# One query against 65,536 keys on one core: second pair's values in three parts, odd pairs' outer stretches in one pass, output rows turned by VectorE

## The chip, the cores and the metric

The kernel runs on one core of a Trainium2 chip. The core has five engines that run side by side and meet through semaphores: TensorE (PE in the profile, with its weight loads as PEld), VectorE (DVE), ScalarE (ACT), GpSimd (POOL) and SyncE (SP). SP does no arithmetic here; it issues the DMA transfers that bring keys and values from device memory (HBM). The transfers are carried by 16 DMA engines. The metric is the device time of one execution in microseconds; lower is better.

## What is computed

The reference is grouped-query attention for a single query position (decode). There are 32 query heads and 8 key/value heads; four query heads share one key/value head.

```python
B, Hq, Hkv, Sq, Sk, D = 1, 32, 8, 1, 65536, 128
k = jnp.repeat(k, 4, axis=1)          # each kv head serves 4 query heads
v = jnp.repeat(v, 4, axis=1)
scores = jnp.einsum("bhqd,bhkd->bhqk", q, k) * D ** -0.5
p = softmax(scores, axis=-1)
out = jnp.einsum("bhqk,bhkd->bhqd", p, v)
```

Keys and values are 134 MB each in bf16 and each byte is used for one small product, so every byte has to be read once: 268.44 MB in all.

## The kernel before, in words

**Units and pairs.** The keys of one head are cut in two halves, and the kernel works on one half at a time. It calls a half a *pair*; there are 16 pairs (`NR`), two per head, numbered i = 0 to 15. A pair has 256 rows of keys per partition (`2 * T`), 8 MiB of keys and 8 MiB of values. It is handled as two units of `A` = 160 and `C` = 96 rows; a unit has its own softmax maximum, and later units rescale the accumulated result.

**The keys of a pair** (`pe_keys`). TensorE transposes the 256 rows in 32 blocks of 8 (L139). VectorE evicts two blocks of three from PSUM to SBUF, ScalarE the third (L240, L238). TensorE multiplies the transposed keys with the queries (L157). As soon as the first 20 blocks have been evicted, `kfree` is raised (L236) and SP may load the next pair's keys. VectorE takes the maximum (L275), GpSimd spreads it over the partitions (L440), ScalarE makes the exponentials (L403).

**The values of a pair** (`pe_values`). TensorE multiplies exponentials and values in three *stretches* (`stretch`, L184): stretch 0 is rows 0 to 96, stretch 1 (the middle one) rows 96 to 160, stretch 2 rows 160 to 256. Each adds up in a PSUM place of its own (`vsum`). Stretch 1 goes first. The two outer stretches follow in a loop of two passes (L200): in even pairs 0 and then 2, in odd pairs 2 and then 0, because the 160-row unit, whose exponentials are ready first, covers stretches 0 and 1 in even pairs and 1 and 2 in odd ones. Ahead of each stretch TensorE waits for a count of `exd` (exponentials done). Each outer stretch raises `pvd`; when both have come, VectorE raises `vfree` (L321), adds the stretches to the accumulator `acc`, and SP may load the next pair's values.

**Small TensorE work in the values.** At the head of `pe_values` TensorE transposes the finished heads' outputs (`oT`, L198), and in the second pass it sums the softmax denominators with a column of ones (L204). Both are done in every pair; only the results of the last pair are used, by VectorE at the end (L381 and L383).

**SyncE's order** (`sync_engine`). Pair 0: keys in three parts, values in one. Pair 1: `load_both(1, 1)`, that is, wait for `kfree`, load the keys, wait for `vfree`, load all values in one transfer (L469 to L473). Pairs 2 to 13: the same in a loop. Pair 14: keys and values in two parts each. Pair 15: keys in three parts, values in eight (`V_PIECES`: 48, 24, 12, 6, 4, 2 rows for stretch 0). There is one value buffer, so a pair's values can be loaded only where the previous pair's have been used. The transfers of SP's queue are carried out in their order of issue. Semaphores `vrdy[0]`, `vrdy[1]` and `vpiece[...]` tell TensorE which part has landed; where a pair is loaded in one transfer, SP raises the others itself.

**The end** (`vector_engine`, L379 to L391). After the last pair VectorE copies the transposed rows of the earlier heads (`orow`), which ScalarE stores; it takes the reciprocal of the denominators, adds stretches 1 and 2, rescales, waits for stretch 0, adds it; TensorE transposes `acc` (L213); VectorE scales it into `olast` (L389), and SP stores it (L502).

Of the kernel before, what the change touches and what calls it, by code (L numbers as in the profile page):

```python
# [5 lines left out]
DT = mybir.dt  # L6
AF = mybir.ActivationFunctionType
ALU = mybir.AluOpType
AX = mybir.AxisListType

P = 128


T = 128
C = 96
A = 2 * T - C
# [25 lines left out]
def take(e, sem, n=1):  # L42

    e.wait_ge(sem, n)
    e.sem_inc(sem, -n)  # L45


def bass_standalone__gqa_softmax__decode_kernel(nc, q, k, v, out):
    _, Hq, _, D = q.shape
    _, H, Sk, _ = k.shape  # L50
    R = Hq // H
    HR = H * R
# [18 lines left out]
    def sb(name, shape, dt):  # L71
        return S(nc.sbuf_tensor(name, shape, dt))

    def sem(name):
        return S(nc.semaphore(name))
# [10 lines left out]
    row = sb("row", [P, 32], DT.float32)  # L86
    ident = sb("ident", [P, P], DT.bfloat16)
    identf = sb("identf", [P, P], DT.float32)
    ones = sb("ones", [P, 1], DT.float32)
    cmax = sb("cmax", [P, R], DT.float32)  # L90
    cmaxa = sb("cmaxa", [P, R], DT.float32)
    m = [sb(f"m{i}", [P, R], DT.float32) for i in range(2)]
# [8 lines left out]
    rl = sb("rl", [R, 1], DT.float32)  # L101
    oT = sb("oT", [P, HR], DT.float32)
    otmp = sb("otmp", [P, HR], DT.float32)
    orow = sb("orow", [HR - R, D], DT.bfloat16)
    olast = sb("olast", [R, D], DT.bfloat16)
    dscr = sb("dscr", [P, 2], DT.float32)

# [1 line left out]

    qkb = [S(nc.psum_tensor(f"qkb{i}", [P, (2 - i) * BANK], DT.float32)) for i in range(2)]  # L110
    pvb = S(nc.psum_tensor("pvb", [P, BANK], DT.float32))
    fin, finl = pvb, qkb[1]

    vsum = (qkb[0][:, 2 * BANK - R:2 * BANK], pvb[:, 0:R], pvb[:, R:2 * R])

    krdy = [sem(f"krdy{i}") for i in range(len(K_PARTS))]
    vrdy = [sem(f"vrdy{i}") for i in range(2)]
    vpiece = [sem(f"vpiece{i}") for i in range(len(V_PIECES))]
    kfree, vfree = sem("kfree"), sem("vfree")
    trd, tra, evd, eva = sem("trd"), sem("tra"), sem("evd"), sem("eva")  # L120
    qkd, qrdy, pvd = sem("qkd"), sem("qrdy"), sem("pvd")
    cm, cma, ng, exd, sx, lrd, lra = (sem(n) for n in ("cm", "cma", "ng", "exd", "sx", "lrd", "lra"))
    xd, xa, xg = sem("xd"), sem("xa"), sem("xg")
    q_sem, o_sem, s_x, t_z, t_id, t_if, t_qT = (
        sem(n) for n in ("q_sem", "o_sem", "s_x", "t_z", "t_id", "t_if", "t_qT"))
    s_o, t_row, s_l, t_acc, s_fin, t_last = (
        sem(n) for n in ("s_o", "t_row", "s_l", "t_acc", "s_fin", "t_last"))

# [33 lines left out]
    def pe_keys(pe, i):  # L164
        for j in range(GA + LAG):
            if j < GA:
                pe_transposes(pe, j, C + j * TB)
            if j >= LAG:
                pe_scores(pe, j - LAG)

        with pe.If(i % 2 > 0):
            for j in range(GA, G):
                pe_transposes(pe, j, j * TB - A)
        with pe.If(i % 2 < 1):
            for j in range(GA, G):
                pe_transposes(pe, j, C + j * TB)
        for j in range(GA, G):
            pe_scores(pe, j)

    def stretch(pe, q):  # L180
        a, b = ((0, C), (C, A), (A, 2 * T))[q]
        starts = [sum(V_PIECES[:n]) for n in range(len(V_PIECES))] if q == 0 else []
        for r in range(a, b):
            ins = pe.matmul(vsum[q], lhsT=vbuf[:, r * D:(r + 1) * D], rhs=pts[:, r * R:(r + 1) * R],  # L184
                            start=r == a, stop=r == b - 1)
            if r in starts:
                ins.wait_op(vpiece[starts.index(r)], 16, "sem-ge")
        if q != 1:
            ins.then_inc(pvd, 1)

    def pe_values(pe, i):

        take(pe, vrdy[0], 16)
        take(pe, exd)

        pe.transpose(qkb[0][0:HR - R, 0:P], oT[:, R:HR], identf[:, :]).then_inc(s_o, 1)  # L198
        stretch(pe, 1)
        with pe.Fori(0, 2) as s:  # L200
            take(pe, exd)
            with pe.If(s > 0):

                pe.matmul(finl[0:R, 0:1], lhsT=lp[:, :], rhs=ones[:, :],  # L204
                          start=True, stop=True).then_inc(s_l, 1)
            with pe.If((i + s) % 2 > 0):
                take(pe, vrdy[1], 16)
                stretch(pe, 2)
            with pe.If((i + s) % 2 < 1):
                stretch(pe, 0)  # L210

    def pe_last(pe):
        ins = pe.transpose(fin[0:R, 0:P], acc, identf[:, :])  # L213
# [30 lines left out]
    def own(e, ins, s):  # L244
        ins.then_inc(s, 1)
        take(e, s)

    def chain(e, *steps, settle=True):

        for n, make in enumerate(steps):  # L250
            ins = make()
            if n:
                ins.wait_op(xd, n, "sem-ge")
            if settle or n < len(steps) - 1:
                ins.then_inc(xd, 1)
        if settle:
            take(e, xd, len(steps))
        else:
            e.sem_inc(xd, 1 - len(steps))
        return ins  # L260
# [107 lines left out]
    def vector_engine(e):  # L368
        identities(e)
        e.memset(dm[0][:, :], 0.0)  # L370
        own(e, e.memset(oT[:, :], 0.0), xd)
        e.wait_ge(s_x, 1)
        own(e, e.tensor_copy(qT[:, :], trb[0][:, 0:HR]), xd)
        next_queries(e, t_qT)
        e.sem_inc(qrdy, 1)
        with e.Fori(0, H) as h:
            for i in range(HALVES):
                dve_round(e, i, h)
        chain(e, rescaled(e, NU - 2))  # L379
        e.wait_ge(s_o, NR)  # L380
        e.tensor_copy(orow[:, :], qkb[0][0:HR - R, 0:P]).then_inc(t_row, 1)  # L381
        e.wait_ge(s_l, NR)
        e.reciprocal(rl[:, :], finl[0:R, 0:1])  # L383
        take(e, pvd)
        chain(e, added(e, 1), added(e, 2), rescaled(e, NU - 1))
        ins = added(e, 0)()
        ins.wait_op(pvd, 1, "sem-ge")
        ins.then_inc(t_acc, 1)
        ins = e.tensor_scalar(olast[:, :], fin[0:R, 0:P], rl[:, 0:1], None, ALU.mult)  # L389
        ins.wait_op(s_fin, 1, "sem-ge")  # L390
        ins.then_inc(t_last, 1)  # L391
# [25 lines left out]
    def scalar_engine(e):  # L417
        e.dma_start(qsb[:, :], qf).then_inc(q_sem, 16)
        e.wait_ge(t_z, 1)
        e.activation(dscr[:, 1:2], dscr[:, 0:1], AF.Exp, scale=1.0)  # L420
        with e.Fori(0, H):
            for i in range(HALVES):
                act_round(e, i)
        e.wait_ge(t_row, 1)
        e.dma_start(of[0:HR - R, :], orow[:, :]).then_inc(o_sem, 16)


    def gpsimd_engine(e):
        e.memset(ident[:, :], 0.0)
        e.memset(identf[:, :], 0.0)  # L430
        e.memset(ones[:, :], 1.0)
        e.memset(dscr[:, :], 0.0)
        e.memset(la[:, :], 0.0).then_inc(t_z, 1)
        e.wait_ge(t_z, 1)
        e.partition_all_reduce(cmaxa[:, :], la[:, :], P, bass.bass_isa.ReduceOp.max).then_inc(xg, 1)
        e.wait_ge(xg, 1)
        with e.Fori(0, H):
            for _ in range(HU):
                take(e, cm)
                e.partition_all_reduce(cmaxa[:, :], cmax[:, :], P, bass.bass_isa.ReduceOp.max).then_inc(cma, 1)  # L440
            take(e, lrd)
            e.partition_all_reduce(la[:, :], lp[:, :], P, bass.bass_isa.ReduceOp.add).then_inc(lra, 1)
# [5 lines left out]
    def sync_engine(e):  # L448
        kp, vp = pairs(kf), pairs(vf)

        def cols(a, b):
            return slice(a * D, b * D)

        def load_k(i, odd, split=(0,)):

            for n, f in enumerate(split):
                last = (split + (len(K_PARTS),))[n + 1]
                a, b = K_PARTS[f], (K_PARTS + (2 * T,))[last]
                r = row_tile(odd, a) if b - a < 2 * T else 0
                t = r if odd else C + r  # L460
                e.dma_start(kbuf[:, cols(t, t + b - a)], kp[i][:, cols(r, r + b - a)]).then_inc(krdy[f], 16)
                for x in range(f + 1, last):
                    e.sem_inc(krdy[x], 16)

        def load_v(i, ready, a, b):
            e.dma_start(vbuf[:, cols(a, b)], vp[i][:, cols(a, b)]).then_inc(ready, 16)

        def load_both(i, odd):
            take(e, kfree)  # L469
            load_k(i, odd)  # L470
            take(e, vfree)
            load_v(i, vrdy[0], 0, 2 * T)
            e.sem_inc(vrdy[1], 16)  # L473

        load_k(0, 0, (0, 1, 2))
        load_v(0, vrdy[0], 0, 2 * T)

        for sm in [vrdy[1]] + vpiece:
            e.sem_inc(sm, 16)
        load_both(1, 1)  # L480
        with e.Fori(1, H - 1) as h:
            load_both(2 * h, 0)
            load_both(2 * h + 1, 1)
        i = NR - 2
        take(e, kfree)
        load_k(i, 0, (0, 2))
        take(e, vfree)
        load_v(i, vrdy[0], 0, A)
        load_v(i, vrdy[1], A, 2 * T)
        i = NR - 1  # L490
        take(e, kfree)
        load_k(i, 1, (0, 1, 2))
        take(e, vfree)
        for sm in vpiece:
            e.sem_inc(sm, -16)
        load_v(i, vrdy[0], C, 2 * C)
        load_v(i, vrdy[1], 2 * C, 2 * T)
        r = 0
        for n, sm in zip(V_PIECES, vpiece):
            load_v(i, sm, r, r + n)  # L500
            r += n
        ins = e.dma_start(of[HR - R:HR, :], olast[:, :])  # L502
        ins.wait_op(t_last, 1, "sem-ge")
        ins.then_inc(o_sem, 16)
        e.wait_ge(o_sem, 32)
# [35 lines left out]
```

## Time and profile before

| | us |
|---|---|
| three runs: median (lowest to highest) | 632.05 (631.78 to 632.28) |
| the profiled execution, its own time | 632.92 |
| its span, first to last instruction | 630.9 |
| busy in the span: PE | 497.2 |
| PEld | 490.3 |
| DVE | 283.4 |
| ACT | 235.5 |
| POOL | 16.5 |

The profile comes from one execution. Its own time is 2.0 us longer than its span, which begins with the first instruction and ends with the last; the 2.0 us lie outside of what the profile shows. The mean clock granted to TensorE was 0.763 of full speed. HBM was read at 425 GB/s over the span. In timeline rows the first number is the start in us from the span's start, the second the length of the row (of all its instructions together), and the bracket at the end gives how long the engine sat idle before it and what ended the wait ("PEq" and "DVEq" are the engine's own sequencer, "issue" a wait for nothing that the profile shows). In rows of DMA issues the last number is the time from issue to landing.

### The profile page before, as it was taken

How to read it: one execution, taken by the hardware profiler on the slowest of the kernel's cores; microseconds unless marked ns; L12 is line 12 of the kernel's file. 1: busy time of each engine (PE TensorE's matmuls, PEld its weight loads, DVE VectorE, ACT ScalarE, POOL GpSimd, SP SyncE). 2: the span in 40 equal slices, each digit the busy share in tenths (PEclk: the TensorE clock that was granted, in tenths of full speed). 3: DMA queues.
4: the chain of work that ended last, by engine and by line, in shares of the span. 5: the costliest groups of instructions: out<-in, count | busy, mean ns of one | idle time of the engine just before them, and what ended most of it. 6: DMA issues, size and time to landing. Idle time of an engine off the chain costs nothing. (4 is left out here: it accounts for less than half of the span.)

```text
span 630.9 us, 27120 instructions
## 1 busy us (share of the span) xinstructions
PE 497.2 (79%) x12338; PEld 490.3 (78%) x12338; DVE 283.4 (45%) x661; ACT 235.5 (37%) x466; POOL 16.5 (3%) x50
## 2 busy tenths in 40 slices
PE   4764994949859498695976969679596895989897
PEld 4664984949859498694976969679596885989897
DVE  4340553615536054461733517355172543646363
ACT  2240441604425044251533515335152451625353
POOL 0000000000000000000000000000000000000000
PEclk9775886958869588695966859678596786958697
DMA  9998999999999999999999999999999999999996
GB/s 376 437 439 352 465 399 465 399 465 399 461 403 461 403 465 399 465 399 465 399 465 399 465 415 449 432 432 445 420 449 415 461 403 461 395 446 417 432 424 284
DMA packets 6587, 268.59 MB, mean 426 GB/s; under 512 B 818, under 2 KB 1202, under 8 KB 1458
## 3 DMA queue, kind: packets, MB, share of 16 engines
q1 hardware_dynamic: 6488, 268.44, 98.8%
q8 instruction: 7, 0.11, 0.1%
q10 hardware_dynamic: 90, 0.02, 0.0%
q14 instruction: 2, 0.02, 0.0%
HBM read 268.44 MB, written 0.01 MB: 425 GB/s over the span
## 5 line engine op out<-in xcount | busy, mean ns | idle before, releaser
L139 PE MATMUL trb<-ident,kbuf 128*128 128x128 bf16 x4096 | 304.1, 237 | 94.3 <-PEq L45 88.6
L139 PEld LDWEIGHTS trb<-ident,kbuf 128*128 128x128 bf16 x4096 | 272.0, 108 | 95.8 <-issue 95.4
L238 ACT ACTIVATE ktb<-trb 128x1024 bf16<-128x1024 bf16 x176 | 180.2, 1024 | 354.3 <-PE trb L139 347.8
L240 DVE COPY ktb<-trb 128x1024 bf16<-128x1024 bf16 x336 | 221.9, 688 | 157.9 <-PE trb L139 154.3
L157 PE MATMUL qkb<-qcur,ktb 128*128 128x4 bf16 x4096 | 132.4, 164 | 0.7 <-issue 0.7
L157 PEld LDWEIGHTS qkb<-qcur,ktb 128*128 128x128 bf16 x4096 | 124.6, 96 | 0.8 <-issue 0.8
L184 PEld LDWEIGHTS pvb<-pts,vbuf 128*128 128x128 bf16 x2560 | 71.0, 102 | 9.4 <-issue 9.2
L184 PE MATMUL pvb<-pts,vbuf 128*128 128x4 bf16 x2560 | 71.9, 166 | 8.1 <-PEq L45 4.8
L184 PE MATMUL qkb<-pts,vbuf 128*128 128x4 bf16 x1536 | 43.4, 166 | 12.6 <-issue 12.6
L184 PEld LDWEIGHTS qkb<-pts,vbuf 128*128 128x128 bf16 x1536 | 42.2, 104 | 14.0 <-issue 14.0
L403 ACT ACTIVATE pts<-qkb,negm 128x160 bf16<-128x160 f32 (+1 forms) x128 | 52.0, 549 | 0.0
L275 DVE TENSOR_REDUCE cmax<-qkb 128x4 f32<-128x640 f32 (+1 forms) x32 | 22.1, 691 | 58.8 <-DVEq L45 58.8
L403 ACT ACTIVATION_READ_ACCUMULATOR pts<-qkb,negm 128x1 f32 x128 | 34.2, 267 | 0.0
L440 POOL PARTITION_ALL_REDUCE cmaxa<-cmax x32 | 12.0, 376 | 580.3 <-POOLq L45 580.3
L325 DVE COPY acc<-qkb 128x4 f32<-128x4 f32 x8 | 1.3, 162 | 46.4 <-DVEq L45 46.4
L314 DVE TENSOR_TENSOR acc<-acc,pvb 128x4 f32<-128x4 f32 x32 | 5.0, 157 | 32.1 <-DVEq L45 31.3
L397 ACT ACTIVATE alpha<-dm 128x4 f32<-128x4 f32 x32 | 6.4, 201 | 32.0 <-ACTq L45 32.0
L303 DVE TENSOR_TENSOR lp<-lp,alpha 128x4 f32<-128x4 f32 x24 | 3.9, 163 | 26.9 <-DVEq L45 26.9
L198 PE MATMUL qkb<-identf,oT 128*28 128x128 f32 x16 | 4.3, 270 | 6.2 <-PEq L45 6.2
L292 DVE TENSOR_TENSOR m<-m,cmaxa 128x4 f32<-128x4 f32 x24 | 3.8, 160 | 8.8 <-DVEq L45 8.8
L198 PEld LDWEIGHTS qkb<-identf,oT 128*28 128x28 f32 x16 | 1.5, 93 | 7.2 <-issue 7.2
L204 PE MATMUL qkb<-ones,lp 128*4 128x1 f32 x32 | 3.0, 163 | 4.6 <-PEq L45 3.9
(44 smaller groups left out, 42.2 us busy)
## 6 DMA issues: line engine op xcount, KB each, us to landing
kbuf<-in_k_dram SPq DMA_DIRECT2D x5, 3072.0 KB, 24.1
vbuf<-in_v_dram SPq DMA_DIRECT2D x2, 3072.0 KB, 22.2
kbuf<-in_k_dram SPq DMA_DIRECT2D x1, 5120.0 KB, 18.3
vbuf<-in_v_dram SPq DMA_DIRECT2D x1, 5120.0 KB, 19.1
kbuf<-in_k_dram SPq DMA_DIRECT2D x2, 2048.0 KB, 12.2
vbuf<-in_v_dram SPq DMA_DIRECT2D x1, 2048.0 KB, 23.0
vbuf<-in_v_dram SPq DMA_DIRECT2D x1, 1536.0 KB, 26.2
vbuf<-in_v_dram SPq DMA_DIRECT2D x1, 768.0 KB, 27.6
```

What stands on the lines that cost most here:

```text
L139: ins = pe.transpose(trb[j % NTB][:, i * P:(i + 1) * P], kbuf[:, t * D:(t + 1) * D], ident[:, :])
L157: ins = pe.matmul(bank[:, t * R:(t + 1) * R], lhsT=ktb[:, off:off + P], rhs=qcur[:, :], start=True, stop=True)
L184: ins = pe.matmul(vsum[q], lhsT=vbuf[:, r * D:(r + 1) * D], rhs=pts[:, r * R:(r + 1) * R], start=r == a, stop=r == b - 1)
L198: pe.transpose(qkb[0][0:HR - R, 0:P], oT[:, R:HR], identf[:, :]).then_inc(s_o, 1)
L238: ins = e.activation(dst, trb[j % NTB][:, :], AF.Copy).then_inc(eva, 1)
L240: ins = e.tensor_copy(dst, trb[j % NTB][:, :]).then_inc(evd, 1)
L275: e.tensor_reduce(cmax[:, :], qkb[part][:, 0:n * R].rearrange("p (t g) -> p g t", g=R), AX.X, ALU.max).then_inc(cm, 1)
L303: chain(e, lambda: e.tensor_tensor(lp[:, :], lp[:, :], alpha[u % 2][:, :], ALU.mult), lambda: e.tensor_tensor(lp[:, :], lp[:, :], rsum[u % ...
L314: return lambda: e.tensor_tensor(acc, acc, vsum[q], ALU.add)
L397: e.activation(alpha[u % 2][:, :], dm[u % 2][:, :], AF.Exp, scale=scale)
L403: ins = e.activation(pv[:, g, r:r + n], sv[:, g, 0:n], AF.Exp, bias=negm[b][:, g:g + 1], scale=scale, accum_out=rsum[b][:, g:g + 1])
L440: e.partition_all_reduce(cmaxa[:, :], cmax[:, :], P, bass.bass_isa.ReduceOp.max).then_inc(cma, 1)
```

## The change

1. **Pair 1's values in three parts.** TensorE raises a new semaphore `vmid` at the end of stretch 1. SP, instead of waiting for the whole of pair 0's values, issues rows 96 to 160 of pair 1's values when `vmid` has come, then waits for `vfree` and issues rows 160 to 256 and rows 0 to 96. Part 0 signals `vpiece[0]`, which SP first takes down by 16.
2. **Odd pairs' outer stretches straight on.** The loop has 2 passes in even pairs and 1 in odd ones; in an odd pair the single pass does stretch 2 and then stretch 0, with a wait for `exd` ahead of each.
3. **Output rows by VectorE.** TensorE's transpose of `oT` (L198) and its sum with the ones (L204) go. After the last pair VectorE turns `oT` in four 32x32 blocks into `orowf`, copies it to `orow`, and makes the reciprocal denominators from `la`, which GpSimd has already summed: a reciprocal, a product with the identity, a sum along the row.

```diff
 def stretch(pe, q):
...
-        if q != 1:
-            ins.then_inc(pvd, 1)
+        return ins

 def pe_values(pe, i):
         take(pe, vrdy[0], 16)
         take(pe, exd)
-
-        pe.transpose(qkb[0][0:HR - R, 0:P], oT[:, R:HR], identf[:, :]).then_inc(s_o, 1)
-        stretch(pe, 1)
-        with pe.Fori(0, 2) as s:
-            take(pe, exd)
-            with pe.If(s > 0):
-                pe.matmul(finl[0:R, 0:1], lhsT=lp[:, :], rhs=ones[:, :],
-                          start=True, stop=True).then_inc(s_l, 1)
+        stretch(pe, 1).then_inc(vmid, 1)
+
+        with pe.Fori(0, 2 - i % 2) as s:
             with pe.If((i + s) % 2 > 0):
                 take(pe, vrdy[1], 16)
-                stretch(pe, 2)
-            with pe.If((i + s) % 2 < 1):
-                stretch(pe, 0)
+                take(pe, exd)
+                stretch(pe, 2).then_inc(pvd, 1)
+            with pe.If(s < 1):
+                take(pe, exd)
+                stretch(pe, 0).then_inc(pvd, 1)

 # vector_engine, after the last pair
-        e.wait_ge(s_o, NR)
-        e.tensor_copy(orow[:, :], qkb[0][0:HR - R, 0:P]).then_inc(t_row, 1)
-        e.wait_ge(s_l, NR)
-        e.reciprocal(rl[:, :], finl[0:R, 0:1])
+        for a in range(0, P, HR):
+            ins = e.transpose(orowf[:, a:a + HR], oT[a:a + HR, :])
+        own(e, ins, xd)
+        e.tensor_copy(orow[:, :], orowf[:, :]).then_inc(t_row, 1)
+        e.wait_ge(lra, 1)
+        chain(e, lambda: e.reciprocal(recip[0:R, :], la[0:R, :]),
+              lambda: e.tensor_tensor(recip[0:R, :], recip[0:R, :], identf[0:R, 0:R], ALU.mult),
+              lambda: e.tensor_reduce(rl[:, :], recip[0:R, :], AX.X, ALU.add))

 # sync_engine
-        load_both(1, 1)
+        take(e, kfree)
+        load_k(1, 1)
+        e.wait_ge(vmid, 1)
+        load_v(1, vrdy[0], C, A)
+        take(e, vfree)
+        e.sem_inc(vpiece[0], -16)
+        load_v(1, vrdy[1], A, 2 * T)
+        load_v(1, vpiece[0], 0, C)
```

The buffer `ones`, its memset on GpSimd and the semaphores `s_o` and `s_l` go as well; ScalarE stores `orow[R:HR, :]`.

More of the change, by code (lines that the diff above doesn't have):

```diff
@@ L88, in bass_standalone__gqa_softmax__decode_kernel @@
     identf = sb("identf", [P, P], DT.float32)
-    ones = sb("ones", [P, 1], DT.float32)
     cmax = sb("cmax", [P, R], DT.float32)
@@ L103, in bass_standalone__gqa_softmax__decode_kernel @@
     otmp = sb("otmp", [P, HR], DT.float32)
-    orow = sb("orow", [HR - R, D], DT.bfloat16)
+    orowf = sb("orowf", [HR, D], DT.float32)
+    orow = sb("orow", [HR, D], DT.bfloat16)
     olast = sb("olast", [R, D], DT.bfloat16)
@@ L111, in bass_standalone__gqa_softmax__decode_kernel @@
     pvb = S(nc.psum_tensor("pvb", [P, BANK], DT.float32))
-    fin, finl = pvb, qkb[1]
+    fin = pvb
     vsum = (qkb[0][:, 2 * BANK - R:2 * BANK], pvb[:, 0:R], pvb[:, R:2 * R])
@@ L118, in bass_standalone__gqa_softmax__decode_kernel @@
     vpiece = [sem(f"vpiece{i}") for i in range(len(V_PIECES))]
-    kfree, vfree = sem("kfree"), sem("vfree")
+    kfree, vfree, vmid = sem("kfree"), sem("vfree"), sem("vmid")
     trd, tra, evd, eva = sem("trd"), sem("tra"), sem("evd"), sem("eva")
@@ L125, in bass_standalone__gqa_softmax__decode_kernel @@
         sem(n) for n in ("q_sem", "o_sem", "s_x", "t_z", "t_id", "t_if", "t_qT"))
-    s_o, t_row, s_l, t_acc, s_fin, t_last = (
-        sem(n) for n in ("s_o", "t_row", "s_l", "t_acc", "s_fin", "t_last"))
+    t_row, t_acc, s_fin, t_last = (
+        sem(n) for n in ("t_row", "t_acc", "s_fin", "t_last"))
     def pe_transposes(pe, j, first):
@@ L424, in scalar_engine @@
         e.wait_ge(t_row, 1)
-        e.dma_start(of[0:HR - R, :], orow[:, :]).then_inc(o_sem, 16)
+        e.dma_start(of[0:HR - R, :], orow[R:HR, :]).then_inc(o_sem, 16)
     def gpsimd_engine(e):
@@ L430, in gpsimd_engine @@
         e.memset(identf[:, :], 0.0)
-        e.memset(ones[:, :], 1.0)
         e.memset(dscr[:, :], 0.0)
```

## The prediction

> **What bounds the kernel now.** I read the page's queue line first, then SyncE's own timeline with the landing times of single issues, then TensorE's timeline where the queue has run out. The page says that the transfer queue is busy nearly all of the span:
>
> ```profile
> span 630.9 us, 27120 instructions
> q1 hardware_dynamic: 6488, 268.44, 98.8%
> ```
>
> So what counts is the stretches in which the queue is empty. Below, SyncE's issues come first (start in us, then the length of the row), and then, in the same order, how long each took to land.
>
> ```profile
> 26.12 0.33 SPq L461 DMA_DIRECT2D kbuf<-in_k_dram  x1
> 62.17 0.33 SPq L466 DMA_DIRECT2D vbuf<-in_v_dram  x1
> 77.30 0.35 SPq L461 DMA_DIRECT2D kbuf<-in_k_dram  x1
> 95.85 0.34 SPq L466 DMA_DIRECT2D vbuf<-in_v_dram  x1
> ```
>
> ```profile
> kbuf<-in_k_dram SPq DMA_DIRECT2D x1, 36.6
> vbuf<-in_v_dram SPq DMA_DIRECT2D x1, 21.9
> kbuf<-in_k_dram SPq DMA_DIRECT2D x1, 26.1
> vbuf<-in_v_dram SPq DMA_DIRECT2D x1, 26.9
> ```
>
> Issue plus landing time gives: pair 1's keys at 62.72, its values at 84.07, pair 2's keys at 103.40, its values at 122.75. From landing to landing the last two steps are 19.33 and 19.35 us: that is what 8 MiB take on a queue that never runs dry. The step before is 21.35. So 2.00 us are lost once, at 62: pair 1's values were issued 0.55 us before the last byte of the keys ahead of them had landed, and DMA engines that were through stood idle. After that every issue comes early: pair 2's keys at 77.30 against a queue busy until 84.07 (6.8 us ahead), its values at 95.85 against 103.40 (7.5 ahead).
>
> At the other end the queue finishes before TensorE. The last piece of pair 15's values is issued at 599.33 and lands 27.7 later, at 627.03, and TensorE's last stretch ends at 625.62 + 2.71 = 628.33; VectorE then waits for nothing else.
>
> ```profile
> 599.33 0.44 SPq L466 DMA_DIRECT2D vbuf<-in_v_dram  x1
> vbuf<-in_v_dram SPq DMA_DIRECT2D x1, 64.0 KB, 27.7
> 619.72 0.27 PE L198 MATMUL qkb<-identf,oT 128*28 128x128 f32 x1 [0.40 <-PEq L45]
> 619.83 1.75 PE L184 MATMUL pvb<-pts,vbuf 128*128 128x4 bf16 x64
> 621.98 2.70 PE L184 MATMUL pvb<-pts,vbuf 128*128 128x4 bf16 x96 [0.40 <-PEq L45]
> 625.09 0.19 PE L204 MATMUL qkb<-ones,lp 128*4 128x1 f32 x2 [0.41 <-PEq L45]
> 625.62 2.71 PE L184 MATMUL qkb<-pts,vbuf 128*128 128x4 bf16 x96 [0.35 <-issue]
> 628.37 0.16 DVE L314 TENSOR_TENSOR acc<-acc,qkb 128x4 f32<-128x4 f32 x1 [2.39 <-PE qkb L184]
> ```
>
> **Part 1, values of pair 1 in three parts.** In pair 0 the middle stretch ends long before 62:
>
> ```profile
> 48.58 1.20 PE L184 MATMUL pvb<-pts,vbuf 128*128 128x4 bf16 x40 [3.32 <-issue]
> 55.91 2.71 PE L184 MATMUL qkb<-pts,vbuf 128*128 128x4 bf16 x96 [6.12 <-issue]
> ```
>
> It is over at 49.78, so the 64 rows are issued near 50, with the keys still running to 62.7. They are a quarter of 8 MiB, 19.35 / 4 = 4.84 us of work, which carries the queue to about 67.5. `vfree` comes near 62.2 as now (a little sooner, since L204 goes), five microseconds before that. The outer parts, issued then, find a busy queue. The gap closes: **-2.00**. What SyncE has waiting behind the new wait on `vmid` is only these values and pair 2's keys, not due before 77.
>
> Three transfers instead of one cost something. The nearest rows are pair 15's keys, which come in the very same sizes:
>
> ```profile
> 561.73 0.43 SPq L466 DMA_DIRECT2D vbuf<-in_v_dram  x1
> vbuf<-in_v_dram SPq DMA_DIRECT2D x1, 3072.0 KB, 26.0
> 576.36 0.43 SPq L461 DMA_DIRECT2D kbuf<-in_k_dram  x1
> kbuf<-in_k_dram SPq DMA_DIRECT2D x1, 3072.0 KB, 30.9
> ```
>
> Pair 14's values are in at 587.73, pair 15's keys at 607.26: 19.53 in three parts against 19.35 in one, **+0.18**. Bounds: 0 to 0.36. The Trainium skill, page "DMA: Bandwidth & Descriptors", section "Anatomy of one DMA — SWDGE (gpsimd) path", gives each transfer of that path a fixed cost of about 2.0 us; two more in series would cost 4.0 and eat the gain. The trace sides against it for queued transfers: the 0.18 above is for two more.
>
> Net of part 1: **-1.8**. Can later stages keep it? Keys and values of pair 2 stay 5 us ahead of a queue that ends 1.8 us sooner, and from there all waits of TensorE are for landings. A lower bound on the gain: the 2.00 is counted on the engine that landed last; the issue at 62.17 came 0.55 before that landing, and if those 0.55 were not lost the gain is 2.00 - 0.55 - 0.18 = 1.3. The new wait for `vpiece[0]` in pair 1 finds its part landed: stretch 0 runs in the last 3 us before 95.85, the part lands near 82.
>
> **Parts 2 and 3, TensorE's path at the end.** These matter only where TensorE doesn't wait for transfers.
>
> ```profile
> 542.69 0.34 SPq L461 DMA_DIRECT2D kbuf<-in_k_dram  x1
> kbuf<-in_k_dram SPq DMA_DIRECT2D x1, 5120.0 KB, 18.3
> 103.56 5.49 PE L139 MATMUL trb<-ident,kbuf 128*128 128x128 bf16 x72 [8.02 <-PEq L45]
> 561.31 6.94 PE L139 MATMUL trb<-ident,kbuf 128*128 128x128 bf16 x72 [0.20 <-PEq L45]
> 592.41 0.19 PE L204 MATMUL qkb<-ones,lp 128*4 128x1 f32 x2 [0.19 <-PEq L45]
> 592.79 2.70 PE L184 MATMUL pvb<-pts,vbuf 128*128 128x4 bf16 x96 [0.20 <-PEq L45]
> 596.00 6.67 PE L139 MATMUL trb<-ident,kbuf 128*128 128x128 bf16 x72 [0.51 <-PEq L45]
> ```
>
> Pair 2's transposes start 0.16 after the landing at 103.40. Pair 14's first keys land at 560.99, but TensorE has just ended pair 13's values (561.31 less 0.20 idle: 561.11) and starts at 561.31. From there it hardly pauses. So the end is a TensorE path from 561, and it gets shorter:
>
> - Pair 13 (odd) loses about 1 us of values (see pair 15), so pair 14 starts when its keys land, 0.16 after 560.99 - 1.8: at 559.35, **-1.96** against now.
> - Pair 14 (even): L198 goes, 0.11 (619.72 to 619.83 in pair 15). L204 and the two pauses around it are 0.19 + 0.19 + 0.20 = 0.58 between the outer stretches; a loop turn, a branch and two waits stay. I take a pause of 0.30, between the 0.20 and the 0.40 that such seams show: **-0.28**. Together -0.39.
> - Pair 15 (odd): L198 again 0.11. From stretch 2's end (624.68) to stretch 0's start (625.62) are 0.94; straight on there remains one branch not taken and one wait, as at 592.79: 0.20. So **-0.74**, bounds -0.54 (a pause of 0.40 stays) and -0.94. Together -0.85.
>
> TensorE would end at 628.33 - 1.96 - 0.39 - 0.85 = 625.13. But the last piece then lands at 627.03 - 1.8 = 625.23, and its two products follow 0.16 later, plus 2 x 0.03 (2.71 / 96): **625.45**. The landing is late next, and the end moves by 628.33 - 625.45 = **-2.88**.
>
> VectorE's new work has to fit beside stretch 0:
>
> ```profile
> 2.06 0.21 DVE L360 STREAM_TRANSPOSE row<-col 128x32 f32<-128x32 f32 x1
> 624.23 0.16 DVE L311 TENSOR_TENSOR acc<-acc,alpha 128x4 f32<-128x4 f32 x1 [0.69 <-DVEq L45]
> 624.54 0.28 DVE L381 CAST orow<-qkb 28x128 bf16<-28x128 f32 x1
> 625.43 0.35 DVE L314 TENSOR_TENSOR acc<-acc,pvb 128x4 f32<-128x4 f32 x2
> ```
>
> The copy at 624.54 starts after pair 15's scores, so it moves by 1.96 + 0.39 to 622.19. From there: four transposes at 0.21 (0.84), a settle 0.15, the copy 0.28, three small steps at 0.2 (the pace of the two at 625.43, rounded up) and a settle (0.75), then the three steps on `acc` that stand there now (0.75): done at 624.96, half a microsecond before 625.45. Hidden; if each of the four transposes took twice as long, 0.84 more, the end would slip by 0.35. The denominators need GpSimd's sum, which the loop makes anyway.
>
> **Sum.** -2.88 at TensorE's end, and what follows it (L314, L213, L389, the store) is unchanged. I round to -2.85: 632.92 - 2.85 = 630.07 for the profiled execution. That execution lay 0.87 above the median of 632.05, so the forecast is 632.05 - 2.85 = **629.2**.
>
> **The rivals.**
>
> *The gap stays* (the early part doesn't reach the queue in time, or a DMA engine's own lag decides). Then only the end is shorter, and the last piece, 0.18 later, bounds it: 627.21 + 0.22 = 627.43, -0.9: **631.15**. Against it: 12 us between 49.78 and 62.17.
>
> *A slow clock in pair 15 eats the end.* Pair 14's last 96 transposes took 7.16, pair 15's 5.52:
>
> ```profile
> 577.09 7.16 PE L139 MATMUL trb<-ident,kbuf 128*128 128x128 bf16 x96
> 611.43 5.52 PE L139 MATMUL trb<-ident,kbuf 128*128 128x128 bf16 x96
> 600.00:602.00 2.00, 2.00 (x27) 2.00 (x26) 0.98 (x3) 1.02 (x1) 0.00 (x0) 0.68 1.00 430
> ```
>
> The granted clock changes inside 600 to 602 (mean 0.68), as the first 72 transposes at 6.67 against 5.49 show. If pair 15 met pair 14's slow stretch, TensorE would end at 625.13 + 1.64 = 626.77, -1.56: **630.5**. The Trainium skill, page "TensorE: Matmul & The Clock Gate", section "What's actually happening", says that the clock is decided in free-running windows of 3413 ns, so that a program shifted by 2 us may meet them otherwise; the rows above fit that, and no row here gives the phase of the next execution.
>
> *Slower: VectorE's tail waits for its code.* The new tail is longer code, run once. TensorE's first passes through its code stand still 3.32 and 6.12 us (rows of pair 0), beside a full queue. A wait of 6.12 there: 624.96 + 6.12 = 631.08 against 628.37 now, +2.7: **634.8**. It decides from 3.4 us on. Against it: today's tail (0.69, then 0.31 to the copy) shows none.
>
> *Slower: each extra part pays a whole start.* An issue into the empty queue landed after 21.9 where the work is 19.35, so 2.55 each. Two in series: +5.1 - 2.0 = +3.1, less 1.1 at the end: **634**. Pair 15's 0.18 speaks against it.
>
> **How the numbers follow.** Forecast 0.75, gap stays 0.06, slow clock 0.11, code wait 0.06, serial starts 0.02. The forecast's own range: -3.4 (a start of the queue 0.5 luckier than the one profiled, since nothing absorbs it any more) to -2.0 (part 1 at 1.3, with VectorE's 0.35): 628.6 to 630.05. The slow clock brings it to 630.5; with it some 0.83 is held, since a little of the forecast's own 0.75 may fall outside. Under 0.2% (1.26 us) a measurement can't tell this kernel from no change: faster 0.87 (forecast, slow clock, a hair of the gap case), same 0.05, slower 0.08.
>
> **What would show it.** Pair 1's values: three issues, the first near 50; the last landing near 82.3, and pair 2's keys near 101.6. If these hold at 84 and 103.4, part 1 has failed. At the end: no pause over 0.3 between the last two stretches, and TensorE's last product right behind the last landing, not after it by more than 0.3. VectorE's wait for TensorE before the last L314 should be near half a microsecond; none there means that its new tail is the bound.

## The result, and the profile after

| | before | after |
|---|---|---|
| median, us (lowest to highest) | 632.33 (630.41 to 633.36), 8 runs | 629.74 (629.64 to 629.98), 8 runs |
| the profiled execution, its own time | 632.92 | 629.64 |
| its span | 630.9 | 627.9 |

The ratio is 0.996, 95% interval [0.9949, 0.9971]: 2.59 us less between the medians, where 2.85 had been forecast. The median itself lies 0.54 above the forecast of 629.2; 0.28 of that is the median of before, 632.33 over these eight runs where the forecast went from 632.05 over three. The scatter has changed as well: the runs of before lie 2.95 us apart, those of after 0.34.

The page of the changed kernel, span and data queue:

```profile
span 627.9 us, 26977 instructions
q1 hardware_dynamic: 6776, 268.44, 99.1%
```

SyncE's timeline after, and the landing times of the single issues in the same order (pair 1's keys, the early part of its values, the last part, pair 2's keys, pair 15's last piece):

```profile
26.06 0.33 SPq L459 DMA_DIRECT2D kbuf<-in_k_dram  x1
49.89 0.33 SPq L464 DMA_DIRECT2D vbuf<-in_v_dram  x1
62.93 0.42 SPq L464 DMA_DIRECT2D vbuf<-in_v_dram  x1
77.17 0.35 SPq L459 DMA_DIRECT2D kbuf<-in_k_dram  x1
594.05 1.54 SPq L464 DMA_DIRECT2D vbuf<-in_v_dram  x1
```

```profile
kbuf<-in_k_dram SPq DMA_DIRECT2D x1, 36.8
vbuf<-in_v_dram SPq DMA_DIRECT2D x1, 2048.0 KB, 17.8
vbuf<-in_v_dram SPq DMA_DIRECT2D x1, 3072.0 KB, 19.4
kbuf<-in_k_dram SPq DMA_DIRECT2D x1, 24.5
vbuf<-in_v_dram SPq DMA_DIRECT2D x1, 64.0 KB, 30.8
```

Pair 1's keys are in at 62.86, its values at 82.33, pair 2's keys at 101.67. From landing to landing that is 19.47 and 19.34: the step that took 21.35 before is an ordinary one now, with some 0.1 for the splitting. The last piece of the kernel lands at 624.85 where it landed at 627.03.

The end after, TensorE's and VectorE's rows:

```profile
617.40 4.53 PE L183 MATMUL pvb<-pts,vbuf 128*128 128x4 bf16 x160 [0.40 <-PEq L45]
621.79 3.29 PE L183 MATMUL qkb<-pts,vbuf 128*128 128x4 bf16 x96
622.23 0.84 DVE L375 STREAM_TRANSPOSE orowf<-oT 32x32 f32<-32x32 f32 x4
624.52 0.16 DVE L305 TENSOR_TENSOR acc<-acc,alpha 128x4 f32<-128x4 f32 x1
625.12 0.16 DVE L308 TENSOR_TENSOR acc<-acc,qkb 128x4 f32<-128x4 f32 x1 [0.44 <-PE qkb L183]
625.52 0.37 PE L207 MATMUL pvb<-identf,acc 128*4 128x128 f32 x1 [0.43 <-DVE acc L308]
```

Stretches 1 and 2 are one row of 160 products and stretch 0 follows without a pause. It takes 3.29 instead of 2.71 because its last products wait for their pieces, and it ends at 625.08, 0.23 after the last landing. VectorE is ready at 624.68 and waits 0.44. Three pauses of before are gone; a pause of 0.43 ahead of L207 has come (0.25 before).

### The profile page after: what moved, and what is told of

It is laid out like the page before. It is cut to its first block, busy times and chain, and to the rows that moved or that the text cites. A ratio compares the mean times of both kernels' runs of the same rounds, so it can differ in the third digit from the quotient of the medians.

```text
span 627.9 us, 26977 instructions
## 1 busy us (share of the span) xinstructions
PE 485.7 (77%) x12290; PEld 480.9 (77%) x12290; DVE 283.7 (45%) x667; ACT 235.4 (37%) x466; POOL 16.4 (3%) x49
## 5 line engine op out<-in xcount | busy, mean ns | idle before, releaser
L139 PE MATMUL trb<-ident,kbuf 128*128 128x128 bf16 x4096 | 298.2, 235 | 112.4 <-PEq L45 106.3
L139 PEld LDWEIGHTS trb<-ident,kbuf 128*128 128x128 bf16 x4096 | 265.9, 106 | 114.0 <-issue 111.7
L305 DVE TENSOR_TENSOR acc<-acc,alpha 128x4 f32<-128x4 f32 x24 | 3.9, 162 | 4.2 <-DVEq L45 3.7
L287 DVE TENSOR_TENSOR dm<-m 128x4 f32<-128x4 f32 x24 | 3.9, 163 | 0.8
L298 DVE TENSOR_TENSOR lp<-lp,rsum 128x4 f32<-128x4 f32 x24 | 3.9, 162 | 0.8
```

Source lines behind the costliest of these rows:

```text
L139: ins = pe.transpose(trb[j % NTB][:, i * P:(i + 1) * P], kbuf[:, t * D:(t + 1) * D], ident[:, :])
L287: lambda: e.tensor_tensor(dm[u % 2][:, :], mo[:, :], mn[:, :], ALU.subtract),
```

## The experiments

The theory: two gains, the empty queue at 62 us (1.8) and TensorE's path at the end (1.0). The main rival: the queue is all of it, because what the end saves is hidden by the last landing anyway. Medians are compared with those of the kernel before beside which each kernel ran; the whole change and the experiments were measured in different sessions.

### The first part alone (e1, and e8 once more)

```diff
 # the kernel before, with only:
+        ins.then_inc(vmid if q == 1 else pvd, 1)
...
-        load_both(1, 1)
+        take(e, kfree); load_k(1, 1); e.wait_ge(vmid, 1)
+        load_v(1, vrdy[0], C, A); take(e, vfree); e.sem_inc(vpiece[0], -16)
+        load_v(1, vrdy[1], A, 2 * T); load_v(1, vpiece[0], 0, C)
```

> The kernel before with the first part of the change alone: pair 1's values in three parts, the middle one when pair 0's middle stretch is done; loop and output rows as before. My theory (the gap at 62 us is worth some 1.8, the shorter TensorE path at the end some 1.0): about 1.8 us under the kernel before, near 630.5, with pair 1's values landing near 82.3 and TensorE's last stretch ending about 1 us behind the last landing. Rival 'the gap is all of it': the same time as the whole change, 629.7. Rival 'the end is all of it': no change from before.

Measured: 629.55 (seven runs, 629.42 to 630.39), before 632.25; ratio 0.9958 [0.9943, 0.9974]. The landing was as expected (60.24 + 22.2 = 82.44), the time was not: the first part alone is as fast as the whole change. The main rival's number came out, mine failed. But the seven runs fall into two groups, four near 629.5 and three at 630.2 to 630.4, so it was measured again:

> The first part of the change alone, a second time. Its runs lay at 629.5 (four) and 630.2 to 630.4 (three). Theory: the upper ones are executions with a 7.16 us stretch of half clock in pair 14 or 15, which the old path at the end (two passes, two more products) can't hide and the new one can; so again two groups some 0.8 us apart, with few runs between, and a profile of the upper group shows such a stretch, one of the lower doesn't. The whole change's runs stay within 0.4 us. Rival: the scatter is chance, and this time it is one group.

Measured: 629.38, 629.38, 629.39, 629.97, 630.36; median 629.39, ratio 0.9962 [0.9949, 0.9975]. The profile of e1 is from the lower group (629.55), that of e8 from the upper one (630.36). TensorE's last 96 transposes of pair 14 and of pair 15, the last stretch, and the final transpose; e1 first:

```profile
575.26 5.53 PE L139 MATMUL trb<-ident,kbuf 128*128 128x128 bf16 x96
608.12 5.52 PE L139 MATMUL trb<-ident,kbuf 128*128 128x128 bf16 x96
622.37 2.83 PE L184 MATMUL qkb<-pts,vbuf 128*128 128x4 bf16 x96 [0.37 <-issue]
625.44 0.38 PE L212 MATMUL pvb<-identf,acc 128*4 128x128 f32 x1 [0.25 <-DVE acc L313]
```

and e8:

```profile
574.86 7.15 PE L139 MATMUL trb<-ident,kbuf 128*128 128x128 bf16 x96
609.08 5.52 PE L139 MATMUL trb<-ident,kbuf 128*128 128x128 bf16 x96
623.28 2.71 PE L184 MATMUL qkb<-pts,vbuf 128*128 128x4 bf16 x96 [0.35 <-issue]
626.24 0.37 PE L212 MATMUL pvb<-identf,acc 128*4 128x128 f32 x1 [0.25 <-DVE acc L313]
```

That the longer row is a clock at half speed is seen in the three microseconds from 575 on, e1 first (the bracketed counts are instructions, first those of TensorE; the third number from the end is the granted clock):

```profile
575.00:578.00 3.00, 3.00 (x62) 2.97 (x59) 2.54 (x4) 1.32 (x2) 0.37 (x1) 1.00 0.89 382
575.00:578.00 3.00, 3.00 (x31) 3.00 (x30) 1.93 (x3) 1.02 (x1) 0.37 (x1) 0.50 0.78 336
```

The last piece lands at the same time in both (595.77 + 29.2 = 624.97 in e1; 624.95 by the landing records of e8). In e8 pair 14 holds 1.62 us of half clock more, and the last stretch starts 0.91 later and ends 1.04 behind the landing; in e1 it ends 0.23 behind it. So in these two profiles the old path at the end reaches the last landing when the clock is kind, and ends some 0.8 later when it isn't. That the other runs of each group are like its one profile is likely but not shown; one run of the twelve, 629.97, lies between the groups.

### The change without its first part (e2, and e10 once more)

```diff
 # the changed kernel, with pair 1's values as before:
+        load_both(1, 1)
-        take(e, kfree)
...
-        load_v(1, vpiece[0], 0, C)
```

> The whole change without its first part: pair 1's values in one transfer once pair 0's are used up. My theory: the gap at 62 stays, and the end moves until the last landing bounds it, about 1.0 us under before (631.3), 1.5 to 1.8 above the whole change. Rival 'the gap is all of it': the time of before, 632.3. Further: if the gap's length is set by how pair 0's values run, and that varies from run to run, the runs of this kernel scatter over 2 to 3 us like those of before, while kernels with the early part stay within 0.5 us.

Measured: 631.99 (12 runs, 631.51 to 632.57), before 632.25; ratio 0.9995 [0.9985, 1.0005]. The end is worth 0.26 of the expected 1.0, and that can't be told from nothing. From here to the whole change (measured in another session) the median falls by 2.25: that is the first part's worth beside the new end. The expected scatter of 2 to 3 us didn't show; the runs lie within 1.06. So the gap alone doesn't make the scatter of before; what does stays open.

Its profile holds something I hadn't allowed for. Pair 1's values were issued at 59.62, a good while before the keys had landed at 62.93 (by the landing records), and still they landed at 84.1:

```profile
59.62 0.33 SPq L464 DMA_DIRECT2D vbuf<-in_v_dram  x1
vbuf<-in_v_dram SPq DMA_DIRECT2D x1, 24.5
623.00 1.44 PE L183 MATMUL qkb<-pts,vbuf 128*128 128x4 bf16 x48 [0.76 <-DMA vbuf<-in_v_dram]
```

The third row is its last stretch, which waits for pieces: in this kernel the last landing bounds the end. By the landing records 15 of the 16 DMA engines had delivered by 82.30 and one at 84.14. The packet records show that one through with its keys at 62.09, idle for 0.73 us, and then taking 4.10 us for its first packet of values, where the other fifteen took 2.42 to 3.32. A second profile:

> The change without its first part, profiled a second time, to see what a late issue loses. In its first profile pair 1's values were issued at 59.62, 0.8 us before the first DMA engine ran dry, and 15 of the 16 engines had landed them by 82.30, one at 84.14. Theory: what is lost is decided per engine, by how far the issue comes ahead of it; with an issue at 62 all engines land near 84 and 2.0 us are lost, with one near 59.6 again most are in time, and the last engine decides. Rival: the late engine was chance, and with the same issue time the landing is near 82.4.

Measured: 631.96 in one run. This time the values of pair 0 lasted longer, the issue came at 62.30, and all 16 engines delivered between 83.50 and 84.07. So the first half of the expectation held; an issue near 59.6 did not come up again, and whether e2's late engine was chance stays open. Its 12 runs, none under 631.5, speak for a loss in each.

### All three parts late (e3)

```diff
-        e.wait_ge(vmid, 1)
+        take(e, vfree)
         load_v(1, vrdy[0], C, A)
-        take(e, vfree)
```

> The whole change, but all three parts of pair 1's values are issued only when pair 0's values are used up. My theory (it is the early issue that counts, the splitting costs 0.18): 0.2 us slower than the same kernel with one transfer, so some 631.5. Rival 'the smaller transfers help by themselves': near the whole change, 629.7.

Measured: 631.82 (12 runs, 631.47 to 632.15), ratio 0.9991 [0.9982, 1.0]. The rival is out: smaller transfers give nothing without the early issue. The expected 0.2 on top of e2 wasn't there (631.82 against 631.99), so the price of splitting, some 0.1 between landings in the changed kernel, doesn't show in the time.

### Small packets in pair 0's values and pair 1's keys (e4)

```diff
 # e2, and:
-        load_v(0, vrdy[0], 0, 2 * T)
+        load_v(0, vrdy[0], C, A); load_v(0, vpiece[0], 0, C); load_v(0, vrdy[1], A, 2 * T)
...
-        load_k(1, 1)
+        load_k(1, 1, (0, 1, 2))
```

> No early part: pair 1's values in one transfer as before, the rest of the change kept; but pair 0's values and pair 1's keys are loaded in three parts each, so their packets are 16 and 24 KB where they were 64 KB. Theory on the cause of the gap: TensorE's first pass through its code waits for code that is fetched over the same DMA engines behind the packets of the data queue (fetches 7.2 us apart, three packets of 2.4 us). With packets of 0.6 to 0.9 us the pauses of 3.3 and 6.1 us in pair 0's values shrink to about 1 and 2.5, the values are used up near 54 to 57 instead of 62, pair 1's values are issued well before the queue runs dry, and the gap closes without the early part: near 629.9 (629.7 plus two more splits at 0.18, the end as in the whole change). Rival 'the pauses in pair 0 have nothing to do with packet size': the gap stays, 631.5.

Measured: 629.89 (629.77 to 630.14), ratio 0.996 [0.9946, 0.9974]: the number came true, the reason didn't. TensorE's rows in pair 0, SyncE's issue of pair 1's values and its landing:

```profile
42.36 0.78 PE L183 MATMUL pvb<-pts,vbuf 128*128 128x4 bf16 x25 [0.20 <-PEq L45]
45.72 1.18 PE L183 MATMUL pvb<-pts,vbuf 128*128 128x4 bf16 x39 [2.58 <-issue]
52.58 2.70 PE L183 MATMUL qkb<-pts,vbuf 128*128 128x4 bf16 x96 [5.68 <-PEq L45]
58.75 0.33 SPq L464 DMA_DIRECT2D vbuf<-in_v_dram  x1
vbuf<-in_v_dram SPq DMA_DIRECT2D x1, 23.7
```

The pauses are 2.58 and 5.68, not 1 and 2.5, and the code packets in the records are still 5.6 to 7.1 us apart. So packet size doesn't set them; the theory on their cause falls, and what sets them stays open. The split had another effect: the part for stretch 1 landed at 28.80, and TensorE began the stretch at 42.36; in e2, with one transfer that landed at 43.57, it waited 2.02 us and began at 43.85. That the issue came earlier for this reason is likely, but no run separates it from the pauses, which vary. The issue came at 58.75, 1.9 us before the first engine had room for it (60.7), and that was enough: the values landed at 82.45, an ordinary step behind the keys (63.06).

### An early part that comes late (e6)

```diff
-        stretch(pe, 1).then_inc(vmid, 1)
+        stretch(pe, 1)      # stretch 0 raises vmid at its 94th row
...
         e.wait_ge(vmid, 1)
-        load_v(1, vrdy[0], C, A)
+        load_v(1, vpiece[0], 0, C - 2)
```

> The whole change, but the early part is issued later: 94 rows of stretch 0, once pair 0's stretch 0 is nearly done (56 to 59 us by how code loading falls out), the rest when all is used. Where the lead before the first DMA engine runs dry (60.5) was 0.8 us, 1.85 us were lost on one engine; where it was 1.9 us (small packets), nothing. Theory 'a lead of some 2 us suffices, what is above it is worth nothing': 629.7 to 630.0 if the issue falls at 56 to 58.5, near 631 in executions in which it falls at 59. Rival 'only an issue long before counts': 631.5 or more throughout.

Measured: 630.05 (629.53 to 630.36), ratio 0.997 [0.9958, 0.9982]. In its profile:

```profile
59.05 0.33 SPq L466 DMA_DIRECT2D vbuf<-in_v_dram  x1
62.48 0.82 SPq L466 DMA_DIRECT2D vbuf<-in_v_dram  x2
vbuf<-in_v_dram SPq DMA_DIRECT2D x1, 2112.0 KB, 12.9
```

The early part left at 59.05, 1.4 us ahead of the first dry engine (60.42), and the last values were in at 82.71 by the landing records, 0.4 later than in the changed kernel. I had expected 631 for such an issue; 630.10 was this execution's time. By the packet records the 0.4 is one engine again: it was through with its keys at 60.84, stood idle until 61.22, and its first packet of values took 2.55 us, where the other fifteen took 0.89 to 1.97. It is one of those that are through early, so little of its delay shows at the last landing; e2's late engine was through only at 62.09. The loss is 2.0 with an issue at 62, 1.8 at 59.62, 0.4 at 59.05 and nothing at 58.75 or 49.9. With a single engine deciding two of these, and packets of different size ahead, I would take no sharp threshold from it.

### The kernel before, profiled again (e5)

> The kernel before, unchanged, profiled a second time. The end of the kernel gave only 0.3 us (measured by the change without its first part) where I had worked out 1.0 from one profile. Theory: that profile held a stretch of half clock in pair 14 (96 transposes in 7.16 us where 5.52 is usual, 1.64 more), which most executions don't hold at the end; without it TensorE's last stretch ends within some 0.3 us of the last landing, and the last three weight-bound stretches wait for landings. So a profile without a 7.16 in pair 14 or 15 shows the last piece landing near 627 and TensorE's end at most 0.5 later. Rival: the distance from last landing to TensorE's end is 1.3 us again without such a stretch; then the shorter path was lost elsewhere.

Measured: 632.38 (12 runs, 631.81 to 633.47); the profiled execution 632.77. It held the half clock again (pair 14's 96 transposes, and the last stretch):

```profile
577.02 7.15 PE L139 MATMUL trb<-ident,kbuf 128*128 128x128 bf16 x96
625.45 2.71 PE L184 MATMUL qkb<-pts,vbuf 128*128 128x4 bf16 x96 [0.35 <-issue]
```

TensorE ends at 628.16, 1.06 behind the last landing. That agrees with the theory but can't test it: the case without was not caught with this kernel. e1 and e8 are the pair that shows it, on the same path at the end.

### Without the last 24 rows (e7)

```diff
-        for n, sm in zip(V_PIECES, vpiece):
+        for n, sm in zip(V_PIECES[:2], vpiece):   # the four small pieces are not loaded
...
+        for sm in vpiece[2:]:
+            e.sem_inc(sm, 16)
```

> The whole change, leaving out the load of the last 24 rows of pair 15's values (the four smallest pieces): the products use what pair 14 left there. Theory 'the last landing bounds the end': the last landing comes about 1.9 us sooner (622.9), TensorE's end follows until its own path bounds it, 0.4 to 0.7 us under the whole change, 629.0 to 629.3. Rival 'TensorE's path bounds the end': the same time, 629.7. Rival 'the queue alone': the full 1.9 us, 627.8.

Measured: 628.98 (628.64 to 629.20), ratio 0.9953 [0.9941, 0.9966], 0.76 under the whole change, which was measured in another session; against the kernels before beside them the two differ by 0.44 (3.03 and 2.59 under before). The last landing bounds the end of the changed kernel, and TensorE takes over as soon as that is 1.9 us earlier: its last 48 products start on a landing and run through.

```profile
623.03 1.44 PE L183 MATMUL qkb<-pts,vbuf 128*128 128x4 bf16 x48 [0.39 <-DMA vbuf<-in_v_dram]
624.73 0.38 PE L207 MATMUL pvb<-identf,acc 128*4 128x128 f32 x1 [0.25 <-DVE acc L308]
```

### The final transpose inside the loop (e9)

```diff
                 stretch(pe, 0).then_inc(pvd, 1)
+                with pe.If(i > NR - 2):
+                    pe_last(pe)
...
-        pe_last(pe)
```

> The whole change, with TensorE's final transpose (L207) moved from behind the two loops into the odd pass, under a branch on the last pair. In the whole change L207 starts 0.43 us after VectorE's last addition, in the first part alone 0.25. Theory: with TensorE waiting for the last landing its sequencer can't run ahead, and the ends of both loops (the inner one's bound is worked out anew, as it depends on the pair) come after the last product; a single branch instead lets the transpose follow in 0.25. So 0.2 us under the whole change, 629.5, and no run near 630.4. Rival: the pause belongs to the accumulator's semaphore, and nothing changes.

Measured: 629.42 (five runs, 629.28 to 629.50), ratio 0.9952 [0.9939, 0.9966]; 0.32 under the whole change of another session, and the two sets of runs don't overlap; against the kernels before beside them it is 0.16 (2.75 and 2.59 under before). Its profile holds the half clock in pair 14, and nothing of it reaches the end:

```profile
574.57 7.15 PE L139 MATMUL trb<-ident,kbuf 128*128 128x128 bf16 x96
625.08 0.16 DVE L309 TENSOR_TENSOR acc<-acc,qkb 128x4 f32<-128x4 f32 x1 [0.80 <-PE qkb L183]
625.29 0.37 PE L209 MATMUL pvb<-identf,acc 128*4 128x128 f32 x1 [0.25 <-DVE acc L309]
```

The pause is 0.25, as expected, 0.18 less than in the whole change. The five runs of e8, the first part alone, have nearly the same median (629.39), but reach up to 630.36.

## Why the prediction was right, and where its terms were off

The direction, the size and the first step were right. Two terms of the sum were wrong in opposite ways: the queue's -1.8 was too small and the end's -1.05 too large. That the sum came out near is in part luck.

1. **"The gap closes."** Right. The early part left at 49.89 (forecast: near 50), the last values landed at 82.33 (82.3), pair 2's keys at 101.67 (101.6). e3 shows that it is the early issue and not the splitting.
2. **"Net of part 1: -1.8."** Too small: 2.25 from e2 to the whole change, 2.70 (before to e1) with the old end. The profiles account for 1.74 at pair 1's values (84.07 to 82.33) and 2.18 at the last piece (627.03 to 624.85). The other 0.4 was lost between 84 and 627 in the profiled execution of before; from pair 1's values to the last piece it took 543.0 us, the other complete kernels with the gap 542.7 to 543.0, those without 542.5 to 542.6. Why a kernel with the gap goes on losing a little there wasn't tested.
3. **"So the end is a TensorE path from 561."** This is the step that failed. It was read from one execution with a stretch of 7.16 us in pair 14, and I priced such a stretch as a rival in pair 15 without asking what the one already in the row was worth. Without it (e1) the old path ends 0.23 behind the last landing and there is nothing to win; with it (e8) some 0.8. Five more profiles hold the slow stretch in pair 14: by the landing records TensorE ends 1.25 and 1.06 behind the last landing with the old end (before, e5; e8 1.04), and 0.25 or 0.26 behind it with the new one (e4, e9, e10). In the median the end gave 0.26 and not 1.0.
4. **"The landing is late next."** Right: 625.08 against a last landing at 624.85, forecast 625.45 and 625.23, and e7 moves with the landing. The pause forecast at 0.20 between the last stretches was none at all, and an odd pair's values got shorter by 1.58 (pair 13 from 8.63 to 7.05), where 0.85 to 1 had been forecast. The even pair 14 came out as forecast in sum, 8.98 to 8.54, though its outer stretches lie 0.54 apart and not 0.30.
5. **VectorE's new tail is hidden.** Right: done at 624.68 (0.84 for the four transposes, as worked out), with 0.44 to spare where 0.49 was forecast. No wait for code showed.
6. **The slow clock in pair 15.** It came, in the very profile of the changed kernel:

```profile
574.04 5.53 PE L139 MATMUL trb<-ident,kbuf 128*128 128x128 bf16 x96
607.48 7.15 PE L139 MATMUL trb<-ident,kbuf 128*128 128x128 bf16 x96
608.00:611.00 3.00, 3.00 (x31) 3.00 (x29) 1.93 (x4) 1.02 (x1) 0.37 (x1) 0.50 1.06 456
```

It cost nothing (the third row has the granted clock, 0.50). The forecast of 630.5 had counted a slow stretch twice, as the row that it started from held one in pair 14 already. Pair 14 was 1.63 faster this time, so TensorE even waited for pair 15's keys (1.84 us at 597.93). The Trainium skill, page "TensorE: Matmul & The Clock Gate", section "What's actually happening", has the clock decided in free-running windows; the profiles agree with that in so far as the long stretch falls into pair 14 (before, e4, e5, e8, e9, e10), into pair 15 (after) or into neither (e1, e2, e3, e6, e7).

What parts 2 and 3 bring by these runs, then, is a narrow scatter more than a lower time: 629.64 to 629.98 with them, 629.38 to 630.39 over the twelve runs of e1 and e8. A small loss comes with them: the final transpose starts 0.43 instead of 0.25 after VectorE. e9 takes that back, so the pause lies in the ends of the two loops; that it is the inner one's bound, which depends on the pair and is worked out again, was argued and not shown.

## What to carry to other kernels

Where a queue of transfers is the bound, look for the step between two landings that is longer than its neighbours, and free part of the next buffer early enough that its transfer is issued well before the queue runs dry, here some 2 us or more; the splitting cost some 0.1. Before a path at the end is priced from one profile, look for what in that execution was unusual (here 7.16 against 5.52 for the same 96 transposes), and ask whether the path would still be the bound without it. A shorter path behind a bound may still pay in scatter.

## What the runs showed of the hardware

- **A transfer that is issued shortly before the queue runs dry is late on some engines only.** An issue needs time of its own: where the engines had run dry, the first packet of values started 0.95 us after it (62.17 to 63.12 before, 62.30 to 63.25 in e10). With an issue at 59.62, 15 of 16 engines had delivered by 82.30, the time of the changed kernel's last, and one 1.8 us later (e2); with one at 59.05 again one engine was held up (e6). A transfer has landed when its last engine is through. Why that one engine is late stays open.
- **An early difference between the DMA engines stays.** In the changed kernel the 16 engines deliver pair 0's first keys within 0.53 us of each other and the second part within 1.75; a code packet of 16 KB (0.96 us at 10.24) and the slower data packet behind it (1.41 where 0.92 is usual) lie between, on one engine, which is then 1.2 us behind the next. It doesn't stay alone: with four such packets four engines are behind when pair 0's values land, with eight (one of them of 8 KB) eight are when pair 1's keys land. The spread is 1.78 at the last stretch's first piece, 600 us later; the queue hasn't run dry in between. Before, the pause at 62 wiped it out (1.77 to 0.67). So by an estimate from this spread up to 1.7 us remain for a kernel whose code is loaded before its data; that wasn't tried.
- **The pauses of pair 0's values vary between executions.** The first was 1.3 to 1.7 us in e1, e2, e8 and e9, 2.5 in e3 and e4 (2.45 and 2.58), and 3.3 to 3.8 in before, after, e5, e6, e7 and e10. The second was 5.7 to 6.6 in all. With the small first pause `vfree` brought SyncE's next issue at 59.6 to 60.2, with the large one at 62.2 to 62.6; with the early part neither matters.
